# The output weight of a gated MLP, loaded in another split over the sixteen DMA engines

## The chip, the cores and the metric

The kernel runs on one core of a Trainium2 chip. The metric is the device time of one execution in microseconds (us). Three runs of the kernel before gave 663.15, 663.30 and 663.37 us; the median is 663.3 us.

## What is computed

Two blocks share one normalized input. Block A is one decoding step of attention with 32 heads over a cache of 4096 keys and values for each of 4 sequences. Block B is a small gated MLP. Their outputs and the input are added. Cut to what matters:

```python
# x: (4, 1, 640)  k_cache, v_cache: (4, 32, 4096, 128)  wq: (640, 4096)  wo: (4096, 640)
# w_in: (640, 1728)  w_out: (864, 640)  all bf16
xn = layernorm(x)
q = heads(xn @ wq)
p = softmax(q @ k_cache^T * 128**-0.5)
a = merge(p @ v_cache) @ wo
z = gelu(xn @ w_in)
z1, z2 = z[..., :864], layernorm(z[..., 864:])
b = (z1 * (w_sp * z2 + b_sp)) @ w_out
out = x + a + b
```

The two caches are 268 MB of the 282 MB that are read. `w_out`, the matrix that the change is about, is 1.1 MB: 864 rows of 1280 bytes.

## The kernel before, in words

One buffer `kv` holds five slots of 32 KB on each of the 128 partitions. Everything large is loaded into it by the queue of SyncE (SP). The order of that queue is written out in the code: `wq` (L111), `w_in` (L114), `w_out` (L118 and four pieces in the loop at L128), and then the caches. A unit of the caches is the keys or the values of eight heads of one sequence, 8.4 MB, 64 KB on each partition; there are 16 units of keys and 16 of values. `load_unit` (L160) issues a unit when the two half slots of its place (L140 to L147) are free; some units are cut in two (L148). After the last unit come `wo` pieces (L536), the last of them cut into four (chunks 0 to 3, 4 and 5, 6, and 7), and then the output.

In between, the engines work on what has landed. VectorE transposes keys (L389, eight times a unit), TensorE makes scores (L400), the softmax follows after four units, and TensorE multiplies the probabilities with the values (L474). `emit_proj` (L520) and the last lines (L561 to L577) multiply with `wo` into the PSUM tiles `proj` and `last`; `o_1`, `o_q` and `o_bf` (L565, L569, L580) add them up, and two DMAs write the result.

Block B stands at the front. TensorE makes `z` from `xnT` and `w_in` (L309, L312), ScalarE takes the gelu (L318, L322), VectorE and GpSimd the normalization (L334 to L352), VectorE transposes the product (L353, giving `uT`), and TensorE multiplies it with `w_out` into `proj` (L367).

`w_out` has 13 chunks (`FC`), each a matrix whose rows lie on partitions:

- 4 chunks (`FA`) of 128 rows, 512 rows in all, 5120 bytes on each partition of slot 2 (L118);
- 9 chunks (`FR`) of at most 44 rows, in two buffers of the pool `ktpool`, which later holds the transposed keys. They come in four pieces `RB`, of 224, 20, 84 and 24 rows. A piece is written as `i` groups of four partitions, and the DRAM side of the DMA has `i` as its first dimension (L128).

The number of DMA engines that a DMA uses shows in the trace by the packets: the DMA of 128 partitions has 8 packets for each of 16 engines; the pieces of `i` = 8, 5, 3 and 3 have 4 packets for each of 8, 5, 3 and 3 engines. Each packet is one partition's run of bytes.

Of the kernel before, what the change touches and what calls it, by code (L numbers as in the profile page):

```python
# [8 lines left out]
ACT = mybir.ActivationFunctionType  # L9
ALU = mybir.AluOpType  # L10
AX = mybir.AxisListType
F32 = mybir.dt.float32
BF16 = mybir.dt.bfloat16
# [3 lines left out]
def kernel(  # L17
# [19 lines left out]
    nc = tc.nc  # L37
    P = 128
    B, Sq, D = A_x.shape
    _, H, Sk, Dh = A_k_cache.shape  # L40
    assert Sq == 1 and B == 4 and Dh == P and D % P == 0
    DC = D // P
# [6 lines left out]
    TC = 32  # L49
# [4 lines left out]
    G = HG * B  # L54
    F2 = B_w_in.shape[1]
    Fh = F2 // 2
    FA = 4
    FR = 9
    RB = ((0, 0, 8, 7), (0, 7, 5, 1), (1, 0, 3, 7), (1, 7, 3, 2))
    NRP = 44  # L60
    assert Fh == FA * P + 4 * sum(i * c for _, _, i, c in RB)
    FC = FA + FR
    NOUT = A_wo.shape[1]
    NH = 2
    NO2 = NOUT // NH
# [3 lines left out]
    const = ctx.enter_context(tc.tile_pool(name="const", bufs=1))  # L69
    small = ctx.enter_context(tc.tile_pool(name="small", bufs=2))  # L70

    NKT = max(2 * TC * 32, 7 * NOUT // 2)
    ktpool = ctx.enter_context(tc.tile_pool(name="ktpool", bufs=2))
    ppool = ctx.enter_context(tc.tile_pool(name="ppool", bufs=2))
    ps_s = ctx.enter_context(tc.tile_pool(name="ps_s", bufs=1, space=bass.MemoryType.PSUM))
# [7 lines left out]
    def misc_ps(shape, dtype):  # L83
        misc_ctr[0] += 1
        return ps_m.tile(shape, dtype, tag="misc", name=f"misc{misc_ctr[0]}")
# [5 lines left out]
    def at_slot(i, n, off=0):  # L91
        return kv[:, i * SL + off:i * SL + off + n]
# [19 lines left out]
    n_in = DC * F2  # L112
    w_in = at_slot(2, n_in).rearrange("p (c f) -> p c f", c=DC)
    nc.sync.dma_start(out=w_in, in_=B_w_in.rearrange("(p c) f -> p c f", c=DC))  # L114

    nf = FA * P
    w_out = at_slot(2, FA * NOUT, n_in).rearrange("p (c n) -> p c n", c=FA)
    nc.sync.dma_start(out=w_out, in_=B_w_out[0:nf, :].rearrange("(p c) n -> p c n", p=P))  # L118
    w_rest = []
    for k, n in ((0, 7), (1, 2)):  # L120
        t = ktpool.tile([P, NKT], F32, tag="kT", name=f"w_rest{k}")[:NRP].bitcast(BF16)[:, 0:n * NOUT]
        w_rest.append(t.rearrange("p (c n) -> p c n", c=n))
    nc.gpsimd.memset(w_rest[1].rearrange("p c n -> p (c n)").bitcast(F32), 0.0)
    r_at = [nf]
    for q, c0, ni, n in RB:
        r_at.append(r_at[-1] + 4 * ni * n)
        k = c0 // 7
        nc.sync.dma_start(out=w_rest[k][32 * q:32 * q + 4 * ni, 0:n].rearrange("p c n -> p (c n)"),  # L128
                          in_=B_w_out[r_at[-2]:r_at[-1], :].rearrange("(r i c) n -> i r (c n)", r=4, c=n))

    NB = 32 * FC
    z_at = n_in + FA * NOUT

    seq = [("k", u) for u in range(B)]
    for u in range(NU):
# [16 lines left out]
    def unit(item, t0, t1):  # L152

        s0, s1 = place[item]
        assert s1 == s0 + 1 or t1 <= T // 2 or t0 >= T // 2
        if t0 >= T // 2:
            return at_slot(s1, (t1 - t0) * Dh, t0 * Dh - SL)
        return at_slot(s0, (t1 - t0) * Dh, t0 * Dh)
# [47 lines left out]
    xnT = const.tile([P, DC, 32], BF16)  # L206
# [43 lines left out]
    for q in range(4):  # L250
        nc.gpsimd.tensor_copy(out=SelE[32 * q:32 * q + 32, :, q % 2, :],
                              in_=b8[32 * q:32 * q + 32, 8:8 + HP, None].to_broadcast((32, HP, P // HG)))
# [10 lines left out]
                          in_=ident_f[:].rearrange("p (q x c) -> p q x c", q=2, c=C2))  # L263
# [10 lines left out]
    proj = ps_j.tile([64, 512], F32)  # L274
    RW = NH * B
    for hf in range(NH):
        nc.tensor.matmul(proj[0:32, 0:NO2], lhsT=ident_bf[:XR, 1 - hf:33 - hf],
                         rhs=x_bf[:, hf * NO2:(hf + 1) * NO2], start=(hf == 0), stop=False)
# [4 lines left out]
    for hf in range(2):  # L283
        for c in range(DC):
            for j in range(NG):
                n0 = j * HG * Dh + hf * 512
                nc.tensor.matmul(q4_ps[32 * j:32 * j + 32, hf * 512:hf * 512 + 512], lhsT=xnT[:, c, :],  # L287
                                 rhs=wq[:, c, n0:n0 + 512], start=(c == 0), stop=(c == DC - 1))
# [12 lines left out]


    w_z = w_in.rearrange("p c (a f) -> p c a f", a=2)
    z_ps = misc_ps([P, 2, FA, 32], F32)
    zr_ps = misc_ps([64, 2, 256], F32)
    w_za = w_z[:, :, :, 0:nf].rearrange("p c a (q j i) -> p c q a i j", q=4, j=32)
    for c in range(DC):
        for q in range(4):
            nc.tensor.matmul(z_ps[32 * q:32 * q + 32], lhsT=xnT[:, c, :], rhs=w_za[:, c, q], start=(c == 0), stop=(c == DC - 1))  # L309
        for q in range(2):  # L310
            f0, f1 = r_at[2 * q], r_at[2 * q + 2]
            nc.tensor.matmul(zr_ps[32 * q:32 * q + 32, :, 0:f1 - f0], lhsT=xnT[:, c, :],  # L312
                             rhs=w_z[:, c, :, f0:f1], start=(c == 0), stop=(c == DC - 1))
    z_f = at_slot(2, 2 * 3 * NB, z_at).bitcast(F32).rearrange("p (a n) -> p a n", a=3)
    z_b = at_slot(2, 2 * NB, z_at + 6 * NB).rearrange("p (a n) -> p a n", a=2)
    zT = z_f[:, 0:2, :].rearrange("p a (i j) -> p a i j", j=32)
    nc.gpsimd.memset(z_f[:, 0:2, :], 0.0)
    nc.scalar.activation(out=zT[:, :, 0:FA, :], in_=z_ps[:], func=ACT.Gelu_apprx_tanh)  # L318
    for (q, c0, ni, n), f0, f1 in zip(RB, r_at[:-1], r_at[1:]):
        f0, f1 = f0 - r_at[2 * q], f1 - r_at[2 * q]  # L320
        for a in range(2):
            nc.scalar.activation(out=zT[32 * q:32 * q + 32, a, FA + c0:FA + c0 + n, 0:4 * ni].rearrange("p c (i r) -> p c i r", r=4),  # L322
                                 in_=zr_ps[32 * q:32 * q + 32, a, f0:f1].rearrange("p (r i c) -> p c i r", r=4, c=n),
                                 func=ACT.Gelu_apprx_tanh)

    one_bf = const.tile([1, P], BF16)
    nc.gpsimd.memset(one_bf[:], 1.0)
# [26 lines left out]
    uT = z_b[:, 1, :]  # L354
# [5 lines left out]

    for f0 in range(0, FC, 4):
        for hf in range(NH):
            for fc in range(f0, min(f0 + 4, FC)):
                n = P if fc < FA else NRP
                nb = 32 if fc == 1 and hf == 0 else RW
                u0, r0 = 32 * fc + 1 - hf, 32 * (fc % 2)
                nc.tensor.matmul(proj[r0:r0 + nb, 0:NO2], lhsT=uT[:n, u0:u0 + nb],  # L367
                                 rhs=(w_out[:, fc] if fc < FA else w_rest[(fc - FA) // 7][:, (fc - FA) % 7])[:, hf * NO2:(hf + 1) * NO2],
                                 start=(fc == 1 and hf == 0), stop=False)


# [9 lines left out]
    def emit_K(u, k):  # L381
# [5 lines left out]
        kw = unit(("k", u), t0, t0 + 2 * TC).bitcast(F32).rearrange("p (t w) -> p t w", w=KW)[:, :, 32 * kh:32 * kh + 32]  # L387
        kT = ktpool.tile([P, NKT], F32, tag="kT", name="kT")[:, 0:2 * TC * 32]
        nc.vector.transpose(kT[:].rearrange("p (t r) -> p t r", r=32), kw)  # L389
# [171 lines left out]
    for c, hf in ((0, 0), (1, 0), (0, 1), (1, 1), (2, 0), (2, 1)):  # L561
        p = min(c, 1)
# [49 lines left out]
```

## Time and profile before

| what | us |
|---|---|
| median of three runs | 663.3 |
| profiled execution, first to last instruction (span) | 661.2 |
| difference, outside the span | 2.1 |
| VectorE busy | 372.2 (56%) |
| TensorE matmuls busy | 287.5 (43%) |
| ScalarE, GpSimd busy | 73.6, 67.0 |
| DMA, mean rate over the span | 427 GB/s |

The profile is of one execution. Its span is the time from the first to the last instruction of the program; nothing else of that execution's own time is given, so sums on the span are carried to the median by adding the 2.1 us that lie outside.

Besides the views of instructions, the trace has a record of every DMA packet (start, duration, bytes, queue), 6930 of them, but not its engine. On one engine a packet starts 4 ns before the one ahead of it ends. So the records can be joined end to start, and with the order of the DMAs and their packet sizes they give sixteen streams, one for each DMA engine. Where an instruction fetch comes between (the queues named "instruction", q8 with 16,384 bytes and q14 with 8192 bytes a packet), the stream has a gap of about its duration.

### The profile page before, as it was taken

How to read it: one execution, taken by the hardware profiler on the slowest of the kernel's cores; microseconds unless marked ns; L12 is line 12 of the kernel's file. 1: busy time of each engine (PE TensorE's matmuls, PEld its weight loads, DVE VectorE, ACT ScalarE, POOL GpSimd, SP SyncE). 2: the span in 40 equal slices, each digit the busy share in tenths (PEclk: the TensorE clock that was granted, in tenths of full speed). 3: DMA queues.
4: the chain of work that ended last, by engine and by line, in shares of the span. 5: the costliest groups of instructions: out<-in, count | busy, mean ns of one | idle time of the engine just before them, and what ended most of it. 6: DMA issues, size and time to landing. Idle time of an engine off the chain costs nothing.

```text
span 661.2 us, 5415 instructions
## 1 busy us (share of the span) xinstructions
PE 287.5 (43%) x2247; PEld 106.6 (16%) x2247; DVE 372.2 (56%) x306; ACT 73.6 (11%) x145; POOL 67.0 (10%) x137
## 2 busy tenths in 40 slices
PE   0436656446062555235436065533706244551236
PEld 0211212112011121111112022110202112120113
DVE  2229999766191759718356286764629175971112
ACT  0300000341100000430200000070110000043200
POOL 3600000031200000130300000030110000003300
PEclk9857788669577587676758577875858769766678
DMA  9999999999999999999999999999999999999996
GB/s 372 452 446 420 420 447 438 429 444 417 436 436 433 428 425 437 433 436 445 416 432 433 432 421 450 427 432 429 437 440 433 424 433 416 445 444 429 419 420 285
DMA packets 6930, 282.58 MB, mean 427 GB/s; under 512 B 811, under 2 KB 1091, under 8 KB 1487
## 3 DMA queue, kind: packets, MB, share of 16 engines
q1 hardware_dynamic: 6879, 282.24, 99.0%
q8 instruction: 17, 0.28, 0.2%
q14 instruction: 6, 0.05, 0.0%
q10 hardware_dynamic: 28, 0.01, 0.0%
HBM read 282.24 MB, written 0.01 MB: 427 GB/s over the span
## 4 chain that ended last, share of the span: by engine, by line
DMA 77%; DVE 9%; issue 8%; PE 4%; ACT 0%; SPq 0%; DVEq 0%; ACTq 0%
DMA kv<-in_A_k_cache_dram 46%; DMA kv<-in_A_v_cache_dram 26%; DVE kT L389 8%; PE O L474 4%; DMA kv<-in_A_wo_dram 4%; DMA kv<-in_A_wq_dram 2%; DVE pT_t L456 0%; ACT Zb L437 0%; DVE m L407 0%; ACT p_bf L450 0%; PE S L400 0%; PE misc L411 0%; SPq L128 0%; PE proj L517 0%; DVE o_q L569 0%
## 5 line engine op out<-in xcount | busy, mean ns | idle before, releaser
L389 DVE STREAM_TRANSPOSE kT<-kv 128x2048 f32<-128x2048 f32 x128 | 282.8, 2275 | 128.1 <-DMA kv<-in_A_k_cache_dram 128.1
L400 PE MATMUL S<-kT,QZ 128*32 128x512 bf16 x1024 | 187.1, 498 | 261.9 <-DVE kT L389 261.9
L400 PEld LDWEIGHTS <-QZ 128*32 128x32 bf16 x1024 | 59.8, 110 | 387.5 <-issue 323.2
L474 PE MATMUL O<-kv,Zb 128*32 128x512 bf16 x1024 | 75.0, 458 | 56.4 <-DMA kv<-in_A_v_cache_dram 49.5
L437 ACT ACTIVATE Zb<-pT_t,MkE 32x128 bf16<-32x128 bf16 x120 | 60.8, 507 | 117.6 <-PE O L474 104.6
L483 DVE TENSOR_TENSOR om<-O,Mk 128x512 f32<-128x512 f32 x15 | 10.4, 692 | 93.8 <-PE O L474 93.8
L435 POOL TENSOR_SCALAR Zb<-pT_t,MkE 32x128 bf16<-32x128 bf16 x60 | 43.1, 718 | 138.6 <-PE O L474 126.1
L474 PEld LDWEIGHTS <-Zb 128*32 128x32 bf16 x1024 | 34.0, 113 | 97.3 <-issue 69.6
L450 ACT ACTIVATE p_bf<-S,negmax 128x1024 bf16<-128x1024 f32 x4 | 4.5, 1115 | 403.7 <-DVE negmax L417 403.7
L433 DVE TENSOR_SCALAR Zb<-pT_t,MkE 32x128 bf16<-32x128 bf16 x76 | 25.1, 330 | 2.3
L375 POOL COPY QZ<-qT 32x32 bf16<-32x32 bf16 x16 | 5.0, 315 | 188.9 <-PE S L400 188.4
L484 DVE TENSOR_REDUCE R<-om 128x128 f32<-128x512 f32 x15 | 15.3, 1021 | 0.5
L456 DVE STREAM_TRANSPOSE pT_t<-p_bf 128x1024 bf16<-128x1024 bf16 (+1 forms) x8 | 9.6, 1240 | 5.5 <-ACT p_bf L450 5.5
L461 POOL TENSOR_SCALAR rs<-MkB,rowsum 128x4 f32<-128x4 f32 x4 | 1.2, 299 | 112.7 <-ACT p_bf L450 112.7
L507 POOL MEMSET oT<- 128x66 bf16 x4 | 0.5, 146 | 96.6 <-PE proj L517 96.6
L407 DVE TENSOR_REDUCE m<-S 128x1 f32<-128x1024 f32 x4 | 4.9, 1224 | 6.0 <-PE S L400 6.0
L486 DVE TENSOR_SCALAR R<-O,Mk 128x128 f32<-128x128 f32 x1 | 0.3, 350 | 14.0 <-PE O L474 14.0
L496 PE MATMUL misc<-R,SelX 128*128 128x512 f32 x8 | 4.5, 644 | 7.2 <-DVE R L484 5.5
L287 PE MATMUL q<-kv,xnT 128*32 128x512 bf16 x40 | 4.3, 614 | 6.4 <-DVE xnT L208 6.4
L463 PE MATMUL misc<-rs,SelE 128*128 128x4 f32 x8 | 2.4, 365 | 10.4 <-POOL rs L461 10.4
L191 DVE CAST kv<-kv 8x640 f32<-8x640 bf16 x1 | 0.5, 482 | 10.7 <-DMA kv<-in_A_x_dram 10.7
L499 DVE TENSOR_TENSOR om<-misc,h 128x512 f32<-128x512 f32 x4 | 2.8, 692 | 4.9 <-PE misc L496 4.9
(102 smaller groups left out, 80.0 us busy)
## 6 DMA issues: line engine op xcount, KB each, us to landing
kv<-in_A_k_cache_dram SPq DMA_DIRECT2D x8, 4096.0 KB, 30.5
kv<-in_A_v_cache_dram SPq DMA_DIRECT2D x1, 6144.0 KB
kv<-in_A_wq_dram SPq DMA_DIRECT2D x1, 5120.0 KB
kv<-in_A_wo_dram SPq DMA_DIRECT2D x3, 1280.0 KB
kv<-in_B_w_in_dram SPq DMA_DIRECT2D x1, 2160.0 KB, 19.8
kv<-in_A_v_cache_dram SPq DMA_DIRECT2D x1, 2048.0 KB
kv<-in_B_w_out_dram SPq DMA_DIRECT2D x1, 640.0 KB, 20.9
kv<-in_A_wo_dram SPq DMA_DIRECT2D x1, 640.0 KB
```

What stands on the lines that cost most here:

```text
L375: nc.gpsimd.tensor_copy(out=QZ[r0:r0 + 32, :, :, :, 8 + 8 * hp], in_=qT[32 * g:32 * g + 32, NE * hp:NE * hp + NE].rearrange("p e a b -> p ...
L389: nc.vector.transpose(kT[:].rearrange("p (t r) -> p t r", r=32), kw)
L400: nc.tensor.matmul(S_ps[32 * q:32 * q + 32, i], lhsT=QZ[:, b, 2 * kh + w, e, w0:w0 + 32], rhs=kb[:, i, :, e, :, w], start=(b == 0 and k < ...
L407: nc.vector.tensor_reduce(out=m1[:], in_=S_ps[:].rearrange("p i t m -> p (i t m)"), axis=AX.X, op=ALU.max)
L433: nc.vector.tensor_scalar(out=dst, in0=src, scalar1=mk, scalar2=None, op0=ALU.mult)
L435: nc.gpsimd.tensor_scalar(out=dst, in0=src, scalar1=mk, scalar2=None, op0=ALU.mult)
L437: nc.scalar.activation(out=dst, in_=src, func=ACT.Copy, scale=mk)
L450: nc.scalar.activation(out=p_bf[:, M:M + NP], in_=S_ps[:].rearrange("p i t m -> p (i t m)"), func=ACT.Exp, bias=negmax[:, 0:1], scale=scal ...
L456: nc.vector.transpose(pT_t[:, j0:j1, :], blocks)
L474: nc.tensor.matmul(O_ps[32 * q:32 * q + 32, :, :], lhsT=Zb[b % 2][:, w].rearrange("p h c -> p (h c)"), rhs=vv[:, w * 4 * Dh:(w + 1) * 4 * ...
L483: nc.vector.tensor_tensor(out=om4[:], in0=O_ps[:], in1=Mk4[:, :, None].to_broadcast((P, 4, Dh)), op=ALU.mult)
L484: nc.vector.tensor_reduce(out=R, in_=om4[:].rearrange("p c d -> p d c"), axis=AX.X, op=ALU.add)
```

## The change

`w_out` gets eight chunks of 128 partitions in slot 2, all in one tile `w_out`; nothing of it is in `ktpool` any more. Its rows come in six pieces `PC` and five DMAs, in this order on SP's queue:

| DMA | rows | partitions | bytes a partition | DMA engines |
|---|---|---|---|---|
| pieces 0 and 1 | 352 | 0 to 43 | 10,240 | lowest 11, four partitions each |
| piece 3 | 168 | 64 to 87 | 8960 | lowest 3, eight partitions each |
| piece 5 | 256 | 96 to 127 | 10,240 | 16, two partitions each |
| piece 2 | 80 | 44 to 59 | 6400 | 16, one partition each |
| piece 4 | 8 | 88 to 95 | 1280 | lowest 8, one partition each |

Two memsets clear partitions 32 to 95 of the tile ahead of the loads, one of GpSimd and one of VectorE, each of 32 partitions x 2560 words of 32 bits; the memset of `w_rest` (44 x 640 words) is gone. The first DMA waits for GpSimd's, the second for VectorE's. The fourth and the fifth wait for the same two earlier DMAs as the third and fourth piece did before.

`z` is made in 20 matmuls (four quadrants of up to 256 rows, five chunks of the contraction) where there were 30, the gelu takes 7 instructions where it took 9, the tiles of the normalization are 256 columns wide where they were 416, and the product with `w_out` takes 16 matmuls on 128 partitions where it took 8 on 128 and 18 on 44.

```diff
-    FA = 4
-    FR = 9
-    RB = ((0, 0, 8, 7), (0, 7, 5, 1), (1, 0, 3, 7), (1, 7, 3, 2))
-    NRP = 44
-    FC = FA + FR
+    FC = 8
+    PC = ((0, 0, 0, 32, 0, 8), (1, 0, 0, 12, 0, 8), (1, 12, 0, 16, 0, 5), (2, 0, 3, 8, 0, 7), (2, 24, 0, 8, 0, 1), (3, 0, 0, 32, 0, 8))
+    f_at = [0]
+    for _, _, k, r, _, n in PC:
+        f_at.append(f_at[-1] + max(k, 1) * r * n)
...
-    NKT = max(2 * TC * 32, 7 * NOUT // 2)
+    NKT = 2 * TC * 32
...
-    nf = FA * P
-    w_out = at_slot(2, FA * NOUT, n_in).rearrange("p (c n) -> p c n", c=FA)
-    nc.sync.dma_start(out=w_out, in_=B_w_out[0:nf, :].rearrange("(p c) n -> p c n", p=P))
-    w_rest = []
-    for k, n in ((0, 7), (1, 2)):
-        t = ktpool.tile([P, NKT], F32, tag="kT", name=f"w_rest{k}")[:NRP].bitcast(BF16)[:, 0:n * NOUT]
-        w_rest.append(t.rearrange("p (c n) -> p c n", c=n))
-    nc.gpsimd.memset(w_rest[1].rearrange("p c n -> p (c n)").bitcast(F32), 0.0)
-    r_at = [nf]
-    for q, c0, ni, n in RB:
-        r_at.append(r_at[-1] + 4 * ni * n)
-        k = c0 // 7
-        nc.sync.dma_start(out=w_rest[k][32 * q:32 * q + 4 * ni, 0:n].rearrange("p c n -> p (c n)"),
-                          in_=B_w_out[r_at[-2]:r_at[-1], :].rearrange("(r i c) n -> i r (c n)", r=4, c=n))
+    w_out = at_slot(2, FC * NOUT, n_in).rearrange("p (c n) -> p c n", c=FC)
+    w_words = w_out.rearrange("p c n -> p (c n)").bitcast(F32)
+    nc.gpsimd.memset(w_words[32:64, :], 0.0)
+    nc.vector.memset(w_words[64:96, :], 0.0)
+
+    def load_piece(eng, i, i1=None):
+        q, x0, k, r, c0, n = PC[i]
+        f0, f1 = f_at[i], f_at[(i if i1 is None else i1) + 1]
+        src = B_w_out[f0:f1, :]
+        src = src.rearrange("(r i c) n -> i r (c n)", i=k, c=n) if k else src.rearrange("(x c) n -> x (c n)", c=n)
+        p0, p1 = 32 * q + x0, 32 * q + x0 + (f1 - f0) // n
+        return eng.dma_start(out=w_out[p0:p1, c0:c0 + n].rearrange("p c n -> p (c n)"), in_=src)
+
+    load_piece(nc.sync, 0, 1)
+    for i in (3, 5, 2, 4):
+        load_piece(nc.sync, i)
...
-            nc.tensor.matmul(z_ps[32 * q:32 * q + 32], lhsT=xnT[:, c, :], rhs=w_za[:, c, q], start=(c == 0), stop=(c == DC - 1))
-        for q in range(2):
-            f0, f1 = r_at[2 * q], r_at[2 * q + 2]
+        for q, (f0, f1) in enumerate(fq):
             nc.tensor.matmul(zr_ps[32 * q:32 * q + 32, :, 0:f1 - f0], lhsT=xnT[:, c, :],
                              rhs=w_z[:, c, :, f0:f1], start=(c == 0), stop=(c == DC - 1))
...
-                n = P if fc < FA else NRP
-                nc.tensor.matmul(proj[r0:r0 + nb, 0:NO2], lhsT=uT[:n, u0:u0 + nb],
-                                 rhs=(w_out[:, fc] if fc < FA else w_rest[(fc - FA) // 7][:, (fc - FA) % 7])[:, hf * NO2:(hf + 1) * NO2],
+                nc.tensor.matmul(proj[r0:r0 + nb, 0:NO2], lhsT=uT[:, u0:u0 + nb], rhs=w_out[:, fc, hf * NO2:(hf + 1) * NO2],
                                  start=(fc == 1 and hf == 0), stop=False)
```

More of the change, by code (lines that the diff above doesn't have):

```diff
@@ L56 @@
     Fh = F2 // 2
-    FA = 4
-    FR = 9
-    RB = ((0, 0, 8, 7), (0, 7, 5, 1), (1, 0, 3, 7), (1, 7, 3, 2))
-    NRP = 44
-    assert Fh == FA * P + 4 * sum(i * c for _, _, i, c in RB)
-    FC = FA + FR
+    FC = 8
[3 more added lines that the diff above has]
+        f_at.append(f_at[-1] + max(k, 1) * r * n)
+    assert Fh == f_at[-1]
     NOUT = A_wo.shape[1]
@@ L114 @@
     nc.sync.dma_start(out=w_in, in_=B_w_in.rearrange("(p c) f -> p c f", c=DC))
-    nf = FA * P
-    w_out = at_slot(2, FA * NOUT, n_in).rearrange("p (c n) -> p c n", c=FA)
-    nc.sync.dma_start(out=w_out, in_=B_w_out[0:nf, :].rearrange("(p c) n -> p c n", p=P))
-    w_rest = []
-    for k, n in ((0, 7), (1, 2)):
-        t = ktpool.tile([P, NKT], F32, tag="kT", name=f"w_rest{k}")[:NRP].bitcast(BF16)[:, 0:n * NOUT]
-        w_rest.append(t.rearrange("p (c n) -> p c n", c=n))
-    nc.gpsimd.memset(w_rest[1].rearrange("p c n -> p (c n)").bitcast(F32), 0.0)
-    r_at = [nf]
-    for q, c0, ni, n in RB:
-        r_at.append(r_at[-1] + 4 * ni * n)
-        k = c0 // 7
-        nc.sync.dma_start(out=w_rest[k][32 * q:32 * q + 4 * ni, 0:n].rearrange("p c n -> p (c n)"),
-                          in_=B_w_out[r_at[-2]:r_at[-1], :].rearrange("(r i c) n -> i r (c n)", r=4, c=n))
+    w_out = at_slot(2, FC * NOUT, n_in).rearrange("p (c n) -> p c n", c=FC)
[12 more added lines that the diff above has]
+        load_piece(nc.sync, i)
     NB = 32 * FC
-    z_at = n_in + FA * NOUT
+    z_at = n_in + FC * NOUT
     seq = [("k", u) for u in range(B)]
@@ L303 @@
     w_z = w_in.rearrange("p c (a f) -> p c a f", a=2)
-    z_ps = misc_ps([P, 2, FA, 32], F32)
-    zr_ps = misc_ps([64, 2, 256], F32)
-    w_za = w_z[:, :, :, 0:nf].rearrange("p c a (q j i) -> p c q a i j", q=4, j=32)
+    zr_ps = misc_ps([P, 2, 256], F32)
+    fq = [(min(f_at[i] for i in range(len(PC)) if PC[i][0] == q), max(f_at[i + 1] for i in range(len(PC)) if PC[i][0] == q)) for q in range(4)]
     for c in range(DC):
-        for q in range(4):
-            nc.tensor.matmul(z_ps[32 * q:32 * q + 32], lhsT=xnT[:, c, :], rhs=w_za[:, c, q], start=(c == 0), stop=(c == DC - 1))
-        for q in range(2):
-            f0, f1 = r_at[2 * q], r_at[2 * q + 2]
+        for q, (f0, f1) in enumerate(fq):
             nc.tensor.matmul(zr_ps[32 * q:32 * q + 32, :, 0:f1 - f0], lhsT=xnT[:, c, :],
@@ L317 @@
     nc.gpsimd.memset(z_f[:, 0:2, :], 0.0)
[L318 to L324, printed above, removed]
+    for (q, x0, k, r, c0, n), f0, f1 in zip(PC, f_at[:-1], f_at[1:]):
+        f0, f1 = f0 - fq[q][0], f1 - fq[q][0]
+        rows = slice(32 * q, 32 * q + 32)
+        dst = zT[rows, :, c0:c0 + n, x0:x0 + max(k, 1) * r]
+        if k == 0:
+            nc.scalar.activation(out=dst, in_=zr_ps[rows, :, f0:f1].rearrange("p a (x c) -> p a c x", c=n), func=ACT.Gelu_apprx_tanh)
+        else:
+            for a in range(2):
+                nc.scalar.activation(out=dst[:, a].rearrange("p c (i r) -> p c i r", r=r),
+                                     in_=zr_ps[rows, a, f0:f1].rearrange("p (r i c) -> p c i r", r=r, c=n),
+                                     func=ACT.Gelu_apprx_tanh)
     one_bf = const.tile([1, P], BF16)
```

## The prediction

> **What bounds the kernel now.** I read the slices first, then the queues, then the chain, then the tail of the timeline.
>
> ```profile
> DMA  9999999999999999999999999999999999999996
> ...
> q1 hardware_dynamic: 6879, 282.24, 99.0%
> q8 instruction: 17, 0.28, 0.2%
> q14 instruction: 6, 0.05, 0.0%
> ...
> DMA 77%; DVE 9%; issue 8%; PE 4%; ACT 0%; SPq 0%; DVEq 0%; ACTq 0%
> ```
>
> The sixteen DMA engines are busy all the time: SP's queue alone takes 99.0% of their span. What the chain calls DVE and issue (17%) is not theirs. The packet records show it: for every one of the 51 loads, the first engine begins it later than SP issued it, by 2.67 us at least (the second unit of values, issued at 134.69, begun at 137.37). No engine ever ran dry. So each engine goes through its own sum of packets, and the end waits for the engine with the largest sum.
>
> ```profile
> 633.07 23.45 DMA kv<-in_A_wo_dram
> 656.52 0.04 issue
> 656.56 0.44 PE proj L517 x4
> ```
>
> That is the chain of waits near its end: the first of the last four `wo` pieces lands at 656.52. It is complete only with its slowest engine.
>
> ```profile
> 657.11 1.37 PE L517 MATMUL last<-kv,oT 128*32 128x160 bf16 x18
> 657.31 0.48 DVE L565 COPY o<-proj 32x320 f32<-32x320 f32 x1 [2.02 <-PE proj L517]
> 657.82 0.65 DVE L569 TENSOR_TENSOR o_q<-proj,o 32x160 f32<-32x160 f32 x2
> 658.57 0.32 DVE L580 TENSOR_TENSOR o_bf<-last,o_q 64x160 bf16<-64x160 f32 x1
> ```
>
> The timeline shows two ends tied at 658.5: VectorE's sums after the landing of 656.52, and the last matmuls after the last landing (658.13 by the semaphore's sixteenth step). Both landings belong to the slowest streams, so a delay of the slowest engine moves the end by as much.
>
> Joined to sixteen streams, the records give these ends of the last data packet, sorted by the pieces of `w_out` that a stream holds:
>
> - engines 0 to 2: 657.15, 657.30, 657.64
> - 3 and 4: 655.28, 656.63
> - 5 to 7: 654.64, 657.59, 657.62
> - 8 to 15 (not told apart): 653.44, 654.11, 656.27, 656.28, 656.31, 656.41, 656.42, 657.73
>
> The spread has two sources: the split of `w_out`, and instruction fetches. A q8 packet (16,384 bytes) stops its stream for 0.97 to 1.08 us and lengthens the next 65,536-byte packet from 2.42 to about 2.9: 1.45 to 1.55 us in all. All 17 fell on eight streams (two of engines 5 to 7, six of 8 to 15); the stream at 657.73 had three.
>
> **The front, at nothing.** Block B gets shorter, but it ends far ahead of what it feeds.
>
> ```profile
> 36.49 2.83 PE L367 MATMUL proj<-w_rest,kv 44*8 44x320 bf16 x18
> ...
> 45.25 15.47 DVE L389 STREAM_TRANSPOSE kT<-kv 128x2048 f32<-128x2048 f32 x7 [10.00 <-DMA kv<-in_A_k_cache_dram]
> ```
>
> The last matmul with `w_out` ends at 39.3; the first transpose of keys begins at 45.25, after 10.00 us of idling for its load. The ten `z` matmuls and ten `w_out` matmuls less, two gelu instructions less, and 256 columns for 416 (GpSimd's four passes of 0.88, 1.76, 0.68 and 1.06 us shrink by about 1.7 us) widen this cover from 6 us. The tile buffers, no longer shared with `w_rest`, are free earlier under the same cover. If it were gone, these edits would gain some 3 to 4 us: 1.7 on GpSimd, and 10 matmuls at L367 at 0.157 us from start to start (2.83/18); DMA issues of that stage have more room (below).
>
> **The memsets.** GpSimd's rows of 128x640 words (0.62 us) and 128x1024 (0.95) give about 2.3 us for 2560 columns, so the first `w_out` DMA is issued near 3.6 us and not at 1.62. VectorE has no memset row; between nothing and the 3.1 us that a reduction would need at the rate of L407 (1.22 us for 1024), it ends before 4.5. The engines reach `w_out` at 19.6, 15 us later. GpSimd's identity tiles, next in its queue, slip by 1.7 us and are wanted at 10.66; ScalarE's table load waits for one of them and has until 14.99. SP's queue stays as it was behind that: the last piece waits until 15.86 for `wq`, as now, and the first keys go out at 16.62. The first engine now takes those up at 21.26; after the change at about 20.7, four microseconds after the issue.
>
> **The split, at full rate.** Packet times from start to start, from this trace: 5120 bytes 0.193 us, 8960 0.334, 1280 0.052, 2560 0.099, 10,240 (`wo`) 0.381; 6400 lies between, 0.241 by its bytes. `w_out` costs an engine:
>
> - 0 to 2: before 8x0.193 + 8x0.334 + 4x0.052 + 4x0.099 = 4.82; after 4x0.381 + 8x0.334 + 2x0.381 + 0.241 + 0.052 = 5.25: +0.43
> - 3 and 4: 3.09 before, 2.58 after: -0.51. 5 to 7: 2.88 and 2.58: -0.30
> - 8 to 10: 1.54 and 2.53: +0.98. 11 to 15: 1.54 and 1.00: -0.54
>
> The latest would be 657.64 + 0.43 = 658.07 against 657.73 now: +0.34 us, unless the stream of 657.73 is one of 8 to 10 (then 658.71, +0.98). Relief of 5 to 7 and 11 to 15 buys nothing once the lowest three are last.
>
> **The split, if engines meet.** What the trace doesn't show is two engines writing the same few partitions at once. Before, a piece gave each engine four partitions and a 128-row load eight. Now sixteen engines write 32 partitions, sixteen write 16, and three engines with eight partitions each write beside engines that load keys. From below the cost is nothing: four partitions an engine ran at full rate (8960 bytes in 0.338 us). A gain is excluded, since no packet of the old pieces ran slower than the stream. From above: the instruction fetch, whose target isn't the streamed partitions, cost its engine 1.5 us for 16,384 bytes that take 0.61 as data, 2.4 times. The input `x` (four engines, four neighbouring partitions, 55 ns for 1280 bytes) doesn't decide: its packets start at 5.47, 5.64, 6.97 and 8.67, never two at once. All sixteen engines hold 27.1 GB/s to within a nanosecond a packet, a fixed ceiling. If it belongs to a group of partitions and not to the engine, two engines there get half each. I take half rate, nearest to the upper row: two sharers make 2, the row has 2.4. On the lowest three that is 2x5.25 = 10.50, +5.68 over 4.82: 657.64 + 5.68 = 663.32, +5.59 on the end. Engines 8 to 10 reach at most 657.73 + 0.98 + 2.53 = 661.24, behind it. With 2.4: 12.60, 665.42, +7.69.
>
> [...]
>
> **Rivals and sums.** Median of before 663.3, span 661.2; the 2.1 us outside stay.
>
> 1. Forecast: engines that write one group of partitions share its rate. 661.2 + 5.59 + 2.1 = **668.9**. For it: the fixed ceiling, and the expensive fetch. Against it: no row of data packets shows a slow one. Chance 0.60; 667 to 671.0 by the bounds.
> 2. They don't share: 661.2 + 0.34 + 2.1 = 663.6, to 664.3 where the stream with three fetches is among 8 to 10. Chance 0.37. For it: four partitions an engine cost no more than eight.
> 3. Faster: one mechanism, the fetches. If the lowest three lose their q14 fetches (some 0.5 to 1 us each) to others because instructions are fewer, engines 5 to 7 end last at 657.62 - 0.30 = 657.32, -0.4 us: 662.9. Even perfect balance (mean of the ends about 656.3) would give 1.4 us, so over 0.2% is nearly out of reach: chance 0.03. It decides from the point where no engine of 0 to 2 holds a fetch and nothing is shared.
>
> Noise: 0.2% is 1.3 us, about what a measurement can tell from no change; rival 2 lies within it. So faster 0.03, same 0.37, slower 0.60. The range must hold both large cases: from 663.2 to 671.0; its two ends leave out the gain and costs over 2.4 times.
>
> **What would show it.** Right: packets of 10,240 and 6400 bytes near 20 to 30 us that last about twice 0.385 and 0.24 us, 8960-byte packets near 0.67, three streams that end over 5 us behind the rest, and a first key unit that lands 5 us after 45.06. Wrong, rival 2: all at 0.385 and 0.338, and a last landing within 1 us of 658.13. Wrong altogether: a stream that runs dry, seen as a gap with no fetch on the stream that ends last, or fetches on other engines.

## The result and the profile after

The changed kernel takes 670.31 us (median of four runs, 669.18 to 671.85), the kernel before 663.34 (663.15 to 663.61): 7.0 us more, a ratio of 1.0107 (95% interval 1.0092 to 1.0121). The profiled execution has a span of 668.6 us where the kernel before has 661.2.

The page of the changed kernel first; it answers to the lines of the queues, the slices and the chain:

```profile
DMA  9999999999999999999999999999999999999996
GB/s 372 301 428 424 439 417 451 439 428 427 436 435 436 423 417 451 429 432 435 436 431 424 435 426 425 444 439 435 425 431 432 439 427 419 458 424 431 429 410 260
...
q1 hardware_dynamic: 6818, 282.24, 98.9%
q8 instruction: 17, 0.28, 0.2%
q14 instruction: 6, 0.05, 0.0%
...
DMA 76%; DVE 10%; issue 10%; PE 3%; SPq 0%; DVEq 0%
```

The DMA engines are as busy as before, with the same bytes and the same 17 and 6 instruction fetches. But "busy" counts a packet from its start to its end, however slowly it moves, so the row of tenths shows nothing. The row of GB/s does: the second slice (16.7 to 33.4 us) falls to 301, from 452 in the kernel before; elsewhere the two rows scatter about the same 430. The row of the kernel before:

```profile
GB/s 372 452 446 420 420 447 438 429 444 417 436 436 433 428 425 437 433 436 445 416 432 433 432 421 450 427 432 429 437 440 433 424 433 416 445 444 429 419 420 285
```

The time was lost in one place, where `w_out` and the first keys are loaded.

The chain of waits (start, length, what) shows the same place and then the end:

```profile
16.26 35.44 DMA kv<-in_A_k_cache_dram
51.70 0.02 issue
51.73 2.37 DVE kT L390 x2
...
639.37 24.52 DMA kv<-in_A_wo_dram
...
663.93 0.44 PE proj L518 x4
```

The first keys land at 51.70, 6.64 us later than before, where the chain has them at 45.06:

```profile
16.62 28.44 DMA kv<-in_A_k_cache_dram
```

From there to the last step for `wo` the chain takes 587.67 us, before 588.01. That step is 1.07 us longer (24.52 for 23.45), and the first of the last four `wo` pieces lands at 663.89 instead of 656.52. The tail behind it, from the timeline:

```profile
664.48 1.36 PE L518 MATMUL last<-kv,oT 128*32 128x160 bf16 x18
664.68 0.48 DVE L566 COPY o<-proj 32x320 f32<-32x320 f32 x1 [3.69 <-PE proj L518]
665.19 0.65 DVE L570 TENSOR_TENSOR o_q<-proj,o 32x160 f32<-32x160 f32 x2
665.94 0.32 DVE L581 TENSOR_TENSOR o_bf<-last,o_q 64x160 bf16<-64x160 f32 x1
```

The same four groups as before, each as long as before, all 7.4 us later. The front has more cover than it had, not less:

```profile
34.40 2.32 PE L369 MATMUL proj<-kv 128*8 128x320 bf16 x16 [4.93 <-DVE kv L356]
51.73 4.50 DVE L390 STREAM_TRANSPOSE kT<-kv 128x2048 f32<-128x2048 f32 x2 [17.38 <-DMA kv<-in_A_k_cache_dram]
```

The product with `w_out` ends at 36.7 (before 39.3), and VectorE then idles 17.38 us for the first keys, where it idled 10.00.

The stretch itself, four microseconds at a time. The columns are time, length, busy time with count of PE, PEld, DVE, ACT and POOL, the granted clock, the DMA share and GB/s. The kernel before:

```profile
20.00:24.00 4.00, 4.00 (x54) 2.00 (x46) 1.27 (x2) 0.59 (x1) 3.75 (x17) 1.00 1.32 561
24.00:28.00 4.00, 0.36 (x2) 0.09 (x1) 1.47 (x4) 3.87 (x11) 2.42 (x6) 1.00 0.98 422
28.00:32.00 4.00, 0.59 (x2) 0.50 (x2) 1.02 (x4) 1.98 (x4) 1.29 (x2) 0.57 1.02 442
```

The changed kernel:

```profile
20.00:24.00 4.00, 4.00 (x49) 1.69 (x37) 0.69 (x1) 0.58 (x1) 3.79 (x19) 1.00 1.34 265
24.00:28.00 4.00, 0.05 (x1) 0.00 (x0) 1.57 (x3) 3.90 (x9) 1.88 (x8) 0.80 1.15 243
28.00:32.00 4.00, 0.59 (x2) 0.50 (x2) 1.04 (x5) 2.70 (x4) 1.39 (x3) 0.50 0.88 286
```

A window counts a packet where it starts, so single windows scatter; but three in a row at 243 to 286 GB/s are 56% of the same three before.

The packet records say who is slow. Packet times between 16 and 45 us (ns; least, median, most):

| bytes | before | after |
|---|---|---|
| 8960 | 338, 338, 338 | 536, 675, 1188 |
| 10,240 | (wo: 385) | 385, 766, 1354 |
| 6400 | none | 421, 590, 824 |
| 65,536 (keys) | 2418; two over 2500, beside fetches | up to 6120; 31 over 2500 |

Pieces of `w_out` at half rate were forecast. The last row was not: the first keys, which every engine writes to its own partitions, are slow too. Joined to sixteen streams, the records give what each stream lost (the sum of its packet times over full rate, from 19 to 45 us):

| streams | w_out before | w_out after | lost in w_out and first keys |
|---|---|---|---|
| engines 0 to 2 | 4.85 | 10.57, 11.23, 11.29 | 6.1 to 6.8 us |
| 3 to 7 | 2.9 to 3.1 | 5.06 to 5.45 | 6.0 to 6.2 |
| 8 to 10 | 1.55 | 5.07 to 5.94 | 6.0 to 6.4 |
| 11 to 15 | 1.55 | 1.38 to 1.95 | 5.6 to 6.3 |

All sixteen lost about the same, 6.1 us (mean 6.12), whether they wrote many shared partitions or few.

### The profile page after: what moved, and what is told of

It is laid out like the page before. It is cut to its first block, busy times and chain, and to the rows that moved or that the text cites. A ratio compares the mean times of both kernels' runs of the same rounds, so it can differ in the third digit from the quotient of the medians.

```text
span 668.6 us, 5379 instructions
## 1 busy us (share of the span) xinstructions
PE 292.6 (44%) x2227; PEld 107.2 (16%) x2227; DVE 373.9 (56%) x307; ACT 74.5 (11%) x143; POOL 67.1 (10%) x137
## 4 chain that ended last, share of the span: by engine, by line
DMA 76%; DVE 10%; issue 10%; PE 3%; SPq 0%; DVEq 0%
DMA kv<-in_A_k_cache_dram 55%; DMA kv<-in_A_v_cache_dram 15%; DVE kT L390 10%; DMA kv<-in_A_wo_dram 4%; PE O L475 2%; DMA kv<-in_A_wq_dram 2%; PE S L401 0%; PE proj L518 0%; DVE o_q L570 0%; DVE o L566 0%; SPq L178 0%; DVEq L390 0%; DVE o_bf L581 0%; SPq L128 0%; SPq L170 0%
## 5 line engine op out<-in xcount | busy, mean ns | idle before, releaser
L401 PE MATMUL S<-kT,QZ 128*32 128x512 bf16 x1024 | 193.9, 513 | 263.3 <-DVE kT L390 263.3
L518 PE MATMUL proj<-kv,oT 128*8 128x320 bf16 x54 | 5.0, 324 | 2.5 <-DMA kv<-in_A_wo_dram 2.5
```

Source lines behind the costliest of these rows:

```text
L401: nc.tensor.matmul(S_ps[32 * q:32 * q + 32, i], lhsT=QZ[:, b, 2 * kh + w, e, w0:w0 + 32], rhs=kb[:, i, :, e, :, w], start=(b == 0 and k < ...
L518: nc.tensor.matmul(dst[0:nb, 0:n1 - n0], lhsT=state[("oT", g)][:, c0:c0 + nb], rhs=wo_t[g][:, c, n0:n1], start=start, stop=stop)
```

## The experiments

Each kernel was timed beside the kernel before, whose medians there are 663.25 to 663.37 us. Where one adds a load, it goes to a free part of slot 1, and nobody reads it. "Group" means four partitions, and in 0 to 63 also the four 32 further on, as the runs below speak for it.

Two theories stood against each other. **Sharing**: two engines that write one group at the same time get its rate between them; pieces dealt so that an engine writes into another's group are slow. **Size or place**: any additional or small piece, or slot 2, the memsets or the shorter front cost the time.

### One more load, in four shapes

The added lines (the second is the one that differs):

```diff
+    spare = at_slot(1, 8 * NOUT, SL - 8 * NOUT)
+    nc.sync.dma_start(out=spare[64:96, :], in_=B_w_out[0:256, :].rearrange("(r i c) n -> i r (c n)", r=4, c=8))
```

The same 256 rows each time: over 128 partitions (sixteen engines, eight partitions each); over 96 to 127 by sixteen engines, two partitions each, as the changed kernel's piece 5; over 0 to 31 by eight engines, four each; over 64 to 95 by the same eight, as above.

> The kernel before, with 256 rows of w_out read once more into unused space of slot 1, 2560 bytes on each of 128 partitions, after the old pieces and ahead of the first keys; nobody reads them. 16 engines, 8 packets of 2560 bytes each, so 8 x 0.099 = 0.79 us on every engine. Theory (engines that write the same partitions share one stream's rate): no sharing here, since this is the split of the key loads; +0.8 us, packets at 0.10 us. Rival (only the bytes of an engine count): the same, +0.8. This run is the yardstick for the next.

> The same 256 rows, but 10,240 bytes on each of partitions 96 to 127: 16 engines, 2 packets of 10,240 bytes each, the same bytes an engine as with 128 partitions. Rival (only bytes count): 2 x 0.381 = 0.76 us, +0.8, packets at 0.385 us. Theory: packets last twice as long or more, and engines that are already loading keys lose time with them; +1.5 to +3.5 us. [...]

> The same 256 rows on partitions 0 to 31 with the DRAM side in 8 groups, as the old pieces are made: 8 engines, 4 packets of 10,240 bytes each, 4 x 0.381 = 1.52 us on the lowest 8 engines. Theory: four partitions for each engine, those that the engine also writes in the old pieces, so no sharing; packets at 0.385 us; the last of the lowest 8 goes from 657.64 to 659.16, +1.4 us. Rival (only bytes count): the same. Rival (long runs on few partitions are slow in themselves): packets near 0.7 us, +3.

> The same DMA as on partitions 0 to 31, with the same source, engines and packets, but on partitions 64 to 95. Theory: if partitions 64 to 95 are those that engines 8 to 15 write in the 128-partition loads, each of the lowest 8 engines now meets another that is loading keys there: packets of 10,240 bytes at about 0.77 us, keys' packets of 65,536 bytes up to 1.5 us longer, the last of the lowest 8 from 657.64 to 660.7: +2.5 to +3.2 us, and more than with partitions 0 to 31 by about 1.5. Rivals (only bytes count; long runs on few partitions are slow): no difference to partitions 0 to 31.

| partitions, engines | time | ratio, 95% | 10,240-byte packets, median | lost by a stream |
|---|---|---|---|---|
| 0 to 127, sixteen | 663.97 | 1.0007 (0.9997 to 1.0017) | (2560 bytes: 102 ns) | 0.0 |
| 0 to 31, eight | 664.63 | 1.0018 (1.0006 to 1.0031) | 385 ns | 0.0 |
| 64 to 95, eight | 667.74 | 1.0065 (1.004 to 1.009) | 773 ns | 2.9 to 3.4 us |
| 96 to 127, sixteen | 667.22 | 1.0053 (1.0034 to 1.0073) | 629 ns | 3.1 to 3.8 us |

The window from 24 to 28 us, of the load on 0 to 31 and then of that on 64 to 95:

```profile
24.00:28.00 4.00, 1.01 (x9) 0.30 (x3) 1.49 (x3) 3.21 (x11) 1.95 (x8) 0.87 0.98 423
```

```profile
24.00:28.00 4.00, 0.77 (x4) 0.18 (x2) 1.59 (x3) 3.45 (x11) 2.09 (x6) 0.81 1.09 252
```

Only the partitions differ, 0 to 31 or 64 to 95, and the rate falls from 423 to 252 GB/s. Size and shape are innocent; the partitions decide. But both slow runs came out dearer than their ranges, and the last column tells why: engines that had nothing to do with the piece lost as much as those in it. The pairwise part of the theory was in doubt.

### Whose partitions, and who loses

Three more loads of this kind: the eight engines on 32 to 63; and 168 rows by the lowest three engines, eight partitions each as in the changed kernel's piece 3, on 64 to 87 and on 8 to 31.

```diff
+    nc.sync.dma_start(out=spare[32:64, :], in_=B_w_out[0:256, :].rearrange("(r i c) n -> i r (c n)", r=4, c=8))
```

```diff
+    nc.sync.dma_start(out=spare[64:88, 0:7*NOUT], in_=B_w_out[0:168, :].rearrange("(r i c) n -> i r (c n)", r=8, c=7))
```

```diff
+    nc.sync.dma_start(out=spare[8:32, 0:7*NOUT], in_=B_w_out[0:168, :].rearrange("(r i c) n -> i r (c n)", r=8, c=7))
```

The "theory of groups" in what was expected of the two loads of 168 rows is sharing by groups of four partitions, the split that ran at 385 ns a packet on 0 to 31: where two engines meet in one group both get half rate, and no other engine loses.

> The kernel before with one more load, read by nobody: the same 256 rows by the same eight lowest engines, four partitions of 10,240 bytes each, as on partitions 0 to 31 (+1.4 us there, all packets at 0.385 us) and on 64 to 95 (+4.5 us, 0.773), now on partitions 32 to 63. [...] Rival 1 (a 128-row load gives each engine eight neighbouring partitions): partitions 32 to 63 are engines 4 to 7's, so packets near 0.77 us and +4 us or more. Rival 2 (any piece that goes beside key loads is slow): as on 64 to 95, +4.5.

> The kernel before with one more load, read by nobody, in the form of the changed kernel's third piece: 168 rows by the lowest three engines, eight partitions each, 8960 bytes a packet, on partitions 64 to 87. At full rate the three streams get 8 x 0.334 = 2.67 us longer: end +2.6 us. Theory of groups, half rate for the two that meet: packets 0.67 us, three streams +5.3, end +5.2 us; of the others only six engines of the upper half lose, each some 1.3 us while its own group is written: the first keys' 65,536-byte packets exceed 2.418 us by some 8 us in sum. Rival (one crossing slows every engine): the same end, but all thirteen others lose about 2.7 us, some 35 us in sum, and packets of the lower half's engines 3 to 7 rise above 2.5 us as well.

> The kernel before with one more load, read by nobody: the same 168 rows by the same three lowest engines, eight partitions each, 8960 bytes a packet, on partitions 8 to 31 (in the twin run: 64 to 87). Theory of groups: engines 1 and 2 write groups that engines 4 to 7 are loading with keys, engine 0 mostly groups of engines 1 and 2 that are away; so packets of 0.67 us for two engines, end +5.2 us, as in the twin, and engines 4 to 7 lose about 1.3 us each. Rival (only a write that crosses from one half of the partitions, 0 to 63 or 64 to 127, to the other half's is slow): all packets 0.338 us, end +2.6 us, no slow key packet.

- **32 to 63**: 664.72 us, ratio 1.0022 (1.0012 to 1.0031), all 32 packets 385 ns, no stream lost anything (0.5 us beside a fetch). Eight engines kept 385 ns a packet on 32 to 63 as on 0 to 31, so 32 to 63 go with the engines of 0 to 31, and both rivals, with +4 us or more, fail. That p and p + 32 are one engine's fits this run and the kernel before, where the lowest three engines wrote 32 to 43 at 338 ns a packet of 8960 bytes; no run shows it one engine at a time, or for 64 to 127.
- **64 to 87**: 667.55 us, 1.0061 (1.0046 to 1.0076), packets of the piece 365 to 698 ns but for the first ones. The end came 4.2 us later; both readings had 5.2. All sixteen streams lost 2.36 to 2.86 us. The rival of that run holds: one crossing slows every engine. The first keys' packets exceed full rate by 33.1 us in sum (rival 35, pairwise 8).
- **8 to 31**: 667.72 us, 1.0065 (1.0048 to 1.0081), all streams lost 2.43 to 2.90 us. The end came 4.4 us later, where the theory of groups had 5.2 and the rival 2.6. The two halves of the partitions are no matter: it is enough to write groups that other engines are writing.

In the run on 64 to 87 the five streams of engines 3 to 7 are far from the piece, in keys of their own, and yet show first key packets of 4382 to 4678 ns (full rate 2418) while it lasts. The window, of 64 to 87:

```profile
24.00:28.00 4.00, 0.55 (x3) 0.09 (x1) 1.52 (x3) 3.68 (x11) 2.33 (x6) 1.00 1.09 282
```

Three engines of sixteen write out of place, and the whole core's rate falls to two thirds of 422.

### Out of place, but not shared

Does a write out of the engine's own group cost by itself, or only where two meet? A load of 352 rows on partitions 4 to 35, put directly behind the 128-row load, lets engine i write engine i+1's group, and engine 7 the group of engine 0, at nearly the same time.

```diff
+    spare = at_slot(1, 11 * NOUT, SL - 11 * NOUT)
+    nc.sync.dma_start(out=spare[4:36, :], in_=B_w_out[0:352, :].rearrange("(r i c) n -> i r (c n)", r=4, c=11))
     w_rest = []
```

> The kernel before with one more load, read by nobody, issued right behind the 128-row load of w_out, so that the engines reach it nearly together: 352 rows by the lowest eight engines, four partitions of 14,080 bytes each (0.529 us a packet by the stream's rate), on partitions 4 to 35. Engine i then writes the four partitions that are engine i+1's, engine 7 those 32 above engine 0's: every engine writes out of its own group, but no two write the same one, except for the few tenths of a us by which they arrive and leave apart. Theory S (what is slow is two engines at one group at the same time; then every stream slows): nearly all of the 32 packets at 0.529, end +2.0 us, excess of the first keys' 65,536-byte packets over 2.418 us below 8 us in sum. Theory F (a write out of the engine's own group is slow in itself, shared or not): packets about 1.06 us, end +4.5 us, excess some 20 us in sum (eight other streams lose 2.4 us each).

665.44 us, ratio 1.0030 (1.0020 to 1.0040): +2.1 for 4 x 0.524 us of work more. No stream lost anything (0.51 us at most, beside a fetch).

```profile
24.00:28.00 4.00, 0.21 (x2) 0.07 (x1) 0.94 (x3) 3.96 (x11) 0.88 (x1) 1.00 1.09 468
```

At 468 GB/s nothing is slow. To be out of place was free here; what cost time in the runs on 64 to 95 and 64 to 87 was to write a group while its own engine wrote it.

### How many must meet

The same eight partitions (64 to 67 and 96 to 99, taken as one group, which is an assumption: the runs speak for four partitions and those 32 further on in 0 to 63 alone) get 10,240 bytes each, once as eight loads of one row, once as two loads of four rows.

```diff
+    for j, p in enumerate((64, 65, 66, 67, 96, 97, 98, 99)):
+        nc.sync.dma_start(out=spare[p:p + 1, :], in_=B_w_out[8 * j:8 * j + 8, :].rearrange("(p c) n -> p (c n)", p=1))
```

```diff
+    for j, p in enumerate((64, 96)):
+        nc.sync.dma_start(out=spare[p:p + 4, :], in_=B_w_out[32 * j:32 * j + 32, :].rearrange("(p c) n -> p (c n)", p=4))
```

> The kernel before with eight more loads of one row each, read by nobody: 10,240 bytes to each of partitions 64 to 67 and 96 to 99, which are one group in the sense of the runs so far. If each one-row load falls to the lowest engine, this engine writes 8 packets (3.05 us at full rate) to the group of one other engine. Pairwise theory (the prediction's): engine 0 at half rate, end +5.5 to +6 us, and one other stream loses 3 us; all the rest lose nothing (excess of the first keys' packets 3 us in sum). Theory of the whole (two engines at one group slow all sixteen): end the same +5.5 to +6, but all other fifteen lose some 2.5 to 3 us, 38 to 45 us in sum.

> The same 64 rows to the same eight partitions as in the run with one engine, but in two loads of four rows, which four engines share: two packets of 10,240 bytes each, four engines and the owner at one group, 0.76 us an engine at full rate. Pairwise theory: a fifth of the rate for four engines, 3.8 us, end +3.7, one owner loses 3 us, the others nothing. Theory of the whole at half rate: packets 0.77 us, end +2.3, the others lose 0.8 to 1.6 us each, 10 to 25 in sum. Theory of the whole at the pace of the fullest group (all streams advance with the slowest): packets some 1.9 us, all streams lose 3 us or more for the 0.76 us of work, end +4 to +7, excess some 45 us or more in sum.

**One engine**: 669.38 us, 1.0083 (1.0068 to 1.0098), but this run is spoilt as a measure of sharing. Eight more loads on SP's queue made SP wait, and the engines ran dry:

```profile
SPq L133 <- DMA kv<-in_B_w_in_dram: 3.6, 1, 3.6
SPq L133 <- DMA w_rest<-in_B_w_out_dram: 1.7, 2, 1.0
SPq L133 <- DMA kv<-in_B_w_out_dram: 1.3, 1, 1.3
```

```profile
20.00:24.00 4.00, 4.00 (x52) 1.98 (x45) 0.89 (x2) 0.58 (x1) 3.79 (x17) 1.00 0.57 233
```

The first fence is that of the waits of SP's queue (what for: us, times, longest), which the kernel before doesn't have; the second is the window from 20 to 24 us, with a DMA share of 0.57 for 1.32. The first keys were issued at 25.71 for 16.62. So the +6 us are mostly idle DMA engines, and its end says nothing for either theory. One stretch shows something all the same: the keys begin at 26.7, and until 28.06 the one engine's packets run beside them, at 385 ns, full rate. The first key packets of all fifteen other streams, started between 26.70 and 27.33, take 2440 to 3574 ns instead of 2418, and that of the engine itself, at 28.06, 2513: 10.5 us too much in sum. That a single intruder slows everyone isn't shown by this, since the engines start from a standstill here. In the profile of the kernel before, the first packets of `wq`, which share nothing, take 1975 to 2784 ns where the later ones take 1514: 11.9 us too much in sum.

**Four engines**: 667.54 us, 1.0057 (1.0042 to 1.0072). An engine's own work grows by 0.76 us, the end by 4.2; packets of the piece up to 1515 ns, first key packets up to 5898 ns; the streams lost 1.8 to 3.7 us, 2.47 in the mean. This run isn't clean either: SP issued the first keys at 20.91 for 16.62, and the streams of engines 8 to 15 stood still for 0.1 to 1.7 us ahead of them. So the 4.2 us hold some idle time, and a part of what these eight lost may come from the start. The eight streams of engines 0 to 7 did not stand still there and lost 1.8 to 2.4 us. Half rate for all would have been 0.8 to 1.6, so four engines at one group seem to cost more than half rate. The last theory, the pace of the fullest group, comes nearest, with 36.2 us in sum for first keys where it had 45 or more.

```profile
24.00:28.00 4.00, 0.16 (x1) 0.00 (x0) 1.47 (x4) 3.89 (x11) 2.62 (x9) 0.97 0.88 273
```

### The changed kernel, mended in part and whole

In part: piece 3 goes over twelve engines with two partitions each instead of three with eight.

```diff
-    PC = ((0, 0, 0, 32, 0, 8), (1, 0, 0, 12, 0, 8), (1, 12, 0, 16, 0, 5), (2, 0, 3, 8, 0, 7), (2, 24, 0, 8, 0, 1), (3, 0, 0, 32, 0, 8))
+    PC = ((0, 0, 0, 32, 0, 8), (1, 0, 0, 12, 0, 8), (1, 12, 0, 16, 0, 5), (2, 0, 0, 24, 0, 7), (2, 24, 0, 8, 0, 1), (3, 0, 0, 32, 0, 8))
```

> The changed kernel with one piece dealt out otherwise: its 168 rows on partitions 64 to 87 go as 24 rows of partitions over twelve engines, two partitions each, instead of three engines with eight each; which rows lie where follows from it, and all 864 are loaded and used. Pairwise theory: engines 0 to 2 need 6.5 us for w_out instead of 10.5, the last stream is then one of 8 to 10 or 3 to 7, the end moves by some 3 to 4 us towards the kernel before: 666 to 667. Theory of the whole (time lost is the time for which any sharing goes on, half of it for each stream): that time falls from 10.6 to 6.8 us in a sum over the pieces, the end by some 2 us: 668 to 668.5. If all advance with the fullest group, the twelve engines meet more often and it comes out no better than the changed kernel, 670.

667.80 us, 1.0065 (1.0047 to 1.0084) to the kernel before: 2.5 us better than the changed kernel, near the theory of the whole (668 to 668.5), and neither 666 to 667 nor 670. The pace of the fullest group, as it was put there, thus fails. The mean loss of a stream falls from 6.1 to 4.1 us.

Whole: eight chunks, the same front, but each engine in its own groups: 768 rows over 128 partitions, 64 over eight engines on 0 to 31, 32 over four on 32 to 47.

```diff
-    PC = ((0, 0, 0, 32, 0, 8), (1, 0, 0, 12, 0, 8), (1, 12, 0, 16, 0, 5), (2, 0, 3, 8, 0, 7), (2, 24, 0, 8, 0, 1), (3, 0, 0, 32, 0, 8))
+    PC = ((0, 0, 0, 32, 0, 6), (1, 0, 0, 32, 0, 6), (2, 0, 0, 32, 0, 6), (3, 0, 0, 32, 0, 6), (0, 0, 8, 4, 6, 2), (1, 0, 4, 4, 6, 2))
...
-    load_piece(nc.sync, 0, 1)
-    for i in (3, 5, 2, 4):
+    load_piece(nc.sync, 0, 3)
+    for i in (4, 5):
```

> The changed kernel with its eight chunks and its shorter front, but w_out in three loads that never leave an engine's own groups: 768 rows as a load of 128 partitions with 7680 bytes each, 64 rows by eight engines on partitions 0 to 31, 32 rows by four engines on 32 to 47, 2560 bytes each (30 matmuls for z instead of 20, three memsets instead of two; all 864 rows are loaded and used). Rows an engine: 0 to 3: 64, 4 to 7: 56, 8 to 15: 48, where the kernel before has 100, 64, 60 and 32. Theory (the changed kernel's loss is the sharing alone, its front costs nothing): all packets at full rate, the last streams are engines 8 to 15 with 0.77 us more than before (657.73 to 658.5), time 664.0 us. Rival 1 (the front, the memsets or the later queue order cost the changed kernel its 7 us): still 668 or more. Rival 2 (chunks in slot 2 are slow by where they lie): packets above the stream's rate, 666 or more.

664.23 us, 1.0015 (1.0006 to 1.0025): the loss of 7.0 us is down to 0.9, where 0.7 was worked out from the rows of engines 8 to 15. Its `z` takes 30 matmuls again, and it has three memsets. No stream lost more than 0.25 us, and the last packet of `wo` ends at 658.36 (forecast 658.5). The window:

```profile
24.00:28.00 4.00, 0.03 (x1) 0.03 (x1) 0.85 (x3) 3.92 (x10) 2.17 (x6) 0.90 1.21 524
```

Slot 2, the memsets, the eight chunks and the short front are all still there. They cost nothing that can be seen here; the deal of the pieces cost the time. No version tried beats the kernel before.

## Why the prediction was right, and where it was wrong

The number was good: 668.9 forecast, 670.3 measured, inside the range, slower as given the larger chance. Not all of the way there was.

- **The bound.** Right: the engines never run dry, the front is cover, and the end moves with the slowest stream. The first keys came 6.64 us later, the end 7.4 in the profiled execution.
- **The front and the memsets, at nothing.** Right. GpSimd's memset and VectorE's, from the timeline of the changed kernel:

```profile
1.39 2.22 POOL L119 MEMSET kv<- 32x2560 f32 x1
...
1.31 2.19 DVE L120 MEMSET kv<- 32x2560 f32 x1 [1.31 <-PEq L597]
```

  Estimated 2.3 us and between nothing and 3.1. The first keys go out at 16.26, and the mended kernel, with one memset more, ends within 0.2 us of what its `w_out` rows alone give, so the front has no price that shows.
- **Full rate for engines in their own groups (rival 2).** Its arithmetic holds where nothing meets: +1.4 and +1.4 us for 1.52 us of work on 0 to 31 and 32 to 63, and the mended kernel within 0.2 us. For the change itself it fails.
- **Half rate where two engines meet.** Right for the pieces in size: 10,240 bytes in 0.766 us in the median (0.385 to 1.354), engines 0 to 2 in 10.57 to 11.29 us where 10.50 was worked out. It isn't the whole mechanism, since engines 11 to 15, with a small share of the pieces, lost nearly as much.
- **"Engines 8 to 10 reach at most 657.73 + 0.98 + 2.53 = 661.24, behind it."** This step failed, and with it the reading that the price falls only on those who share. Every stream lost 5.6 to 6.8 us. The three engines do not end 5 us behind the rest, as the prediction wanted to see: at the end of the first keys they stand at 50.3 to 51.3 us and the others at 46.0 to 48.3, where before it was 43.9 to 44.6 and 40.6 to 42.1. The gap was there already and grew by less than 1 us in the mean.
- **The sum.** 5.59 us were put on the end: 5.68 for the lowest three at half rate. The term that is missing is the common loss, 6.1 us for each stream, and the split's own part comes on top of it. In the profiled execution the stream furthest behind at 657.9 has the packets of engines 8 to 10 and three q8 fetches (59.9, 359.7 and 654.5 us): 657.73 + 0.98 for the split + 6.1 to 6.4 = 664.8 to 665.1, and the last packet of `wo` ends at 665.06. So the case that rival 2 set aside as its upper end, a stream with three fetches among 8 to 10, is the one that set the end here. That the forecast was near is luck; two errors met: the wrong engines, and a common loss that happens to be as large as what half rate costs the lowest three.
- **Rival 3.** The fetches are still 17 and 6, and nothing was gained.

What the common loss goes by was worked out afterwards, and no further run tested it. Take the packets that come from elsewhere into the fullest group at each time, at their full-rate durations, and add them over the times when different engines arrive:

| run | worked out | lost by a stream, mean |
|---|---|---|
| 64 to 87 and 8 to 31, three engines: 8 x 0.334 | 2.67 | 2.45, 2.50 |
| 64 to 95, eight engines, in two arrivals: 2 x 4 x 0.381 | 3.05 | 3.04 |
| four engines on one group (assumed to be one, and not a clean run), in two arrivals: (2 + 6) x 0.381 | 3.05 | 2.47 |
| 96 to 127, sixteen engines, in three arrivals: 0.76 + 1.52 + 1.52 | 3.8 | 3.28 |
| changed kernel: 1.52 (engines 8 to 10 into the groups of 0 to 2) + 2.67 (piece 3) + 1.52 (piece 5, two into one group) + 0.72 (piece 2) | 6.4 | 6.12 |
| the same with piece 3 over twelve: 1.52 + 1.34 + 1.52 + 0.96 | 5.3 | 4.1 |

It comes out equal or up to 29% too high, and it gets the order of the runs but for the load of four engines on one group. All engines seem to stand still for as long as the fullest group needs for the intruders' bytes. The run with one engine speaks against it rather than for it: 1.36 us of its packets ran beside the first keys, and a stream lost 0.66 us in the mean, which the start from a standstill may explain by itself. Why engines whose partitions nobody else writes should wait isn't settled; no run looked for it.

## What to carry to other kernels

When a load is dealt out to some of the engines by hand, see to it that no two engines write the same group (here four neighbouring partitions and, as the runs on 0 to 63 speak for it, those 32 further on) at the same time: here one piece out of place cost all sixteen engines 2 to 4 us, and the changed kernel's pieces together some 6. Where everything is bound by the DMA engines, first see which of them own the partitions, then balance their bytes; balance bought with sharing is dear. And where a row of busy tenths shows nines, read the rate below it, and the packet times of the loads that were not changed.

## What the runs showed of the hardware

- Engines that wrote groups whose own engines were loading slowed all sixteen streams, by nearly the same amount: 2.4 to 2.9 us with three such engines (64 to 87), 2.9 to 3.4 with eight (64 to 95), 5.6 to 6.8 in the changed kernel. For one such engine it isn't shown.
- Writing into another engine's group cost nothing while that engine was elsewhere: with 352 rows shifted by one group, no stream lost more than 0.51 us, and that beside a fetch.
- Partitions 32 to 63 go with the engines of 0 to 31: eight engines kept 385 ns a packet of 10,240 bytes on both. That p and p + 32 are one engine's fits the runs on 0 to 63; for 64 to 127 nothing shows it.
- In the run on 64 to 87 the first one or two packets of the piece still ran at full rate (338 ns of 8960 bytes), and a single intruder kept 385 ns for 10,240 bytes all the time.
- The first packets of `wq`, which start from a standstill, are slow with nothing shared: 1975 to 2784 ns, where the later ones take 1514.
